# Windowed attention and two feed-forward layers on one core: a scheduled order of issue, 64-key softmax and a first block in halves

## The chip, the core and the metric

One core of a Trainium2 chip runs the whole program in a single launch. The metric is the device time of one execution in microseconds (us), lower is better. Engines are named as in the profile: PE is the tensor engine (PEld its weight loads), DVE the vector engine, ACT the scalar engine, POOL is GpSimd and SP issues most of the DMA transfers.

## What is computed

Three layers follow each other; all inputs and outputs are float32. `w_in` is 512 x 2048, `w_out` 2048 x 512, `w_a` and `w_b` 512 x 1536, and the last `w_out` 1536 x 512.

```python
# q, k, v: (4, 8, 576, 64); a query sees itself and the 63 keys before it
scores = q @ k^T / sqrt(64); scores outside 0 <= i - j < 64 are set to -1e9
attn   = softmax(scores); x = attn @ v, as 2304 tokens x 512
h = x @ w_in;  g = relu(h) ** 2;  x = g @ w_out            # layer 1
a = x @ w_a;   b = x @ w_b;       out = (a * b) @ w_out    # layer 2
```

## The kernel before, in words

**Precision.** Each factor of the two layers is held as a high and a low part in float32r. A product is therefore three matmuls, high x high, high x low and low x high (`mm3`, lines 169 to 172). Attention multiplies in plain float32; the trace shows two MATMUL records for each such matmul.

**Weights.** A tile of 128 x 512 weights arrives as 64-bit words (`w_load`, line 91), and `conv_1` to `conv_3` (lines 107 to 140) turn it into a high and a low part: three instructions on ACT (L119, L120, L138) and four on DVE (L126, L129, L130, L139). There are 68 tiles, two landing buffers, and 14, later 20, slots for converted tiles.

**Layers.** The 2304 tokens are in five blocks, `BLOCKS`, the first of 256 tokens and four of 512. Layer 1 uses its 16 units of 128 hidden columns in two groups (`G1`: 7 and 9), layer 2 its 12 units in two groups of 6 (`G2`). A group goes over all blocks before the next one begins, and a block's partial sums are kept in DRAM between the groups of a layer. `unit1` (line 462) is 12 matmuls into `ps_h`, relu and square on ACT and DVE (lines 363 to 366), and 12 matmuls into four accumulators `acc`. `unit2` (line 493) has two first products, `ps_a` and `ps_b`, and one second. A unit's second product is issued after the first product of the next unit (`pend`).

**Attention.** 128 tokens, a pair of chunks of 64, are one step `k` of `tick` (line 321), 18 in all. `att_scores` (line 229) multiplies 64 x 64 pieces of Q with 128 keys: four heads-pairs `hp`, two heads `j` in a pair and two chunks `e`, so 16 matmuls, into two buffers, one for each `j`. Consecutive matmuls go over the four combinations of `j` (rows 0 to 63 or 64 to 127 of the array) and `e` (its columns):

```python
        for hp in range(NHP):
            for j in range(2):
                r = slice(j * W, (j + 1) * W)
                for e in range(2):
                    o = slice(e * W, (e + 1) * W)
                    nc.tensor.matmul(
                        pss[j][o, hp, :],
                        q_t[c][r, e, hp, :],
                        k_t[c][r, hp, e * W:e * W + P],
```

The mask is added by a bf16 matmul for the first five pairs and on DVE after that. Maximum, exponential (ACT, L272, one instruction for each buffer and `hp`, over 128 keys) and division follow; `att_transpose` (line 289) turns each 128 x 128 piece with the array's transpose, 8 for a pair, copied to SBUF by ACT; `att_values` (line 300) is 16 matmuls of 64 columns.

**Order.** The code is written in a fixed interleaving: three parts of a tick and three parts of a conversion inside each unit. `plan1` (line 530) starts with three units of block 0, then block 1, then the rest of block 0, then blocks 2 to 4. Every engine works through its own queue in the order in which it was built.

Of the kernel before, what the change touches and what calls it, by code (L numbers as in the profile page):

```python
# [27 lines left out]
BLOCKS = [(0, 256), (256, 512), (768, 512), (1280, 512), (1792, 512)]  # L28
G1 = [range(0, 7), range(7, 16)]
G2 = [range(0, 6), range(6, 12)]  # L30
N0 = 3
ORDER = [1, 0, 2, 3, 4]
NPR = NCH // 2
PR = 2 * W
PR0 = BLOCKS[0][1] // PR
# [4 lines left out]
MASK_PE = 5  # L40
# [3 lines left out]
def kernel(  # L44
# [18 lines left out]
    raw_p = ctx.enter_context(tc.tile_pool(name="raw_p", bufs=2))  # L63
# [13 lines left out]


    src = {"in": w_in, "out": w_out, "a": w_a, "b": w_b, "out2": w_out2}
    seq = []  # L80
    last_use = {}
    for gi, (ph, us) in enumerate([(1, G1[0]), (1, G1[1]), (2, G2[0]), (2, G2[1])]):
        for u in us:
            for kind in ("in", "out") if ph == 1 else ("a", "b", "out2"):
                last_use[kind, u] = len(seq)
                seq.append((kind, u))
    n_load, n_conv = [0], [0]
    raw_t, wh, wl, slot_of = {}, {}, {}, {}
    free = [(ring_a, i) for i in range(N_A)]

    def w_load(k=1):
        for _ in range(k):
            if n_load[0] < len(seq) and n_load[0] < n_conv[0] + RAW:
                kind, u = key = seq[n_load[0]]
                n_load[0] += 1
                t = raw_p.tile([P, 512, 2], U32, tag="raw", name="raw", bufs=RAW)
                nc.sync.dma_start(out=t.rearrange("p f w -> p (f w)"), in_=src[kind][u].bitcast(U32))
                raw_t[key] = t
# [6 lines left out]
    cvs = [cv_p]  # L105

    def conv_1():
        if n_conv[0] == len(seq) or not free:
            return None
        key = seq[n_conv[0]]  # L110
        if key not in raw_t:
            w_load()
        n_conv[0] += 1
        slot_of[key] = free.pop(0)
        pool = cvs[n_conv[0] % len(cvs)]
        t = raw_t[key]
        a = pool.tile([P, 512], F32, tag="a", name="a")
        s = pool.tile([P, 512, 2], U16, tag="s", name="s")
        nc.scalar.activation(out=a, in_=t[:, :, 1].bitcast(F32), func=AF.Copy, scale=2.0 ** -112)  # L119
        nc.scalar.activation(out=s[:, :, 0], in_=t[:, :, 0], func=AF.Copy, scale=2.0 ** -29)  # L120
        return key, a, s

    def conv_2(key, a, s):
        t = raw_t.pop(key)
        au = a.bitcast(U32)
        nc.vector.tensor_scalar(  # L126
            out=s[:, :, 1], in0=t.bitcast(U16)[:, :, 3], scalar1=0x8000, scalar2=None, op0=ALU.bitwise_and
        )
        nc.vector.tensor_scalar(out=au, in0=au, scalar1=3, scalar2=None, op0=ALU.logical_shift_left)  # L129
        nc.vector.tensor_tensor(out=au, in0=au, in1=s.rearrange("p f w -> p (f w)").bitcast(U32), op=ALU.add)  # L130
        w_load()
        return key, a

    def conv_3(key, a):
        pool, i = slot_of[key]
        hi = pool.tile([P, 512], F32R, tag=f"wh{i}", name="wh")
        lo = pool.tile([P, 512], F32R, tag=f"wl{i}", name="wl")
        nc.scalar.copy(out=hi, in_=a)  # L138
        nc.vector.tensor_tensor(out=lo, in0=a, in1=hi.bitcast(F32), op=ALU.subtract)  # L139
        wh[key], wl[key] = hi, lo  # L140


    flow = {2: [], 3: []}

    def conv_step(step, k=1):
        for _ in range(k):
            if step == 1:
                r = conv_1()
                if r:
                    flow[2].append(r)  # L150
            elif flow[step]:
                r = flow[step].pop(0)
                if step == 2:
                    flow[3].append(conv_2(*r))
                else:
                    conv_3(*r)

    def need(key):
        while key not in wh:
            if not (flow[2] or flow[3]):  # L160
                conv_step(1)
            conv_step(2)
            conv_step(3)

    def w_done(kinds, u):
        for kind in kinds:
            free.append(slot_of.pop((kind, u)))
# [6 lines left out]
    def proj(ps, key, t):  # L174
        n = BLOCKS[t][1]
        h_, l_ = wh[key], wl[key]
        for kc in range(KC):
            c = slice(kc * P, (kc + 1) * P)
            mm3(ps[:, :n], h_[:, c], l_[:, c], xh[t][:, kc, :], xl[t][:, kc, :], kc == 0, kc == KC - 1)


    att = ExitStack()
    ld_p = att.enter_context(tc.tile_pool(name="ld_p", bufs=2))
# [7 lines left out]

    q_t, k_t, v_t = {}, {}, {}

    def ok(c):
        return 0 <= c < NPR

    def load_qk(c):
        if ok(c):  # L200
# [7 lines left out]
            if lo:  # L208

                nc.gpsimd.memset(k_t[c][:, :, :lo], 0.0)  # L210
# [445 lines left out]
```

## Time and profile before

| what | value |
|---|---|
| three runs | 957.81, 959.85, 960.30 us |
| median | 959.85 us |
| the profiled execution | 959.12 us, span 957.3 us |
| PE busy | 919.5 us (96%) |
| DVE busy, ACT busy | 433.1 us (45%), 382.6 us (40%) |
| DMA moved | 82.46 MB, mean 86 GB/s |

Times below are in one profiled execution, counted from the first instruction. Busy time is time in which an engine holds at least one instruction. Matmuls overlap each other on PE, so a busy PE can still be doing less than it could: the distance between two starts tells its pace.

### The profile page before, as it was taken

To read this page: it belongs to the slowest core of one execution; us is meant where nothing else is said; L and a number is where in the kernel's file an instruction comes from. 1 tells how busy PE (TensorE), PEld (TensorE's weight loads), DVE (VectorE), ACT (ScalarE), POOL (GpSimd) and SP (SyncE) were. 2 spreads that over 40 slices of the span, in tenths; PEclk is the share of its full clock that TensorE was granted. 3 is DMA by queue.
4 is the path that set the end of the run, shared out by engine and by line. 5 is a ranking of instruction groups with operands and counts; after the bars stand their busy time and mean duration, and the time that the engine had idled before them with its cause. 6 is when DMAs were issued, how large, how long until landed. Compare 5 with 4: busy or idle time off the path is not lost.

```text
span 957.3 us, 13306 instructions
## 1 busy us (share of the span) xinstructions
PE 919.5 (96%) x5314; PEld 764.6 (80%) x5314; DVE 433.1 (45%) x803; ACT 382.6 (40%) x866; POOL 2.0 (0%) x11
## 2 busy tenths in 40 slices
PE   4778999999999999999999999999999999999998
PEld 3666787778877898888888898888888888888886
DVE  3587865646885243242798122121484122121222
ACT  4787755556774232232686121111373111111111
POOL 0000000000000000000000000000000000000000
PEclk9899999999999999999999999999999999999999
DMA  6767734222655011010253010010252120002011
GB/s 179 215 197 224 214 116 126 69 89 88 219 175 173 1 39 45 1 45 1 82 193 131 2 45 23 1 45 0 88 166 86 46 83 27 24 22 66 8 48 45
DMA packets 59278, 82.46 MB, mean 86 GB/s; under 512 B 23248, under 2 KB 34896, under 8 KB 59216
## 3 DMA queue, kind: packets, MB, share of 16 engines
q1 hardware_dynamic: 58816, 81.41, 27.0%
q8 instruction: 42, 0.69, 0.3%
q10 hardware_dynamic: 400, 0.20, 0.1%
q14 instruction: 20, 0.16, 0.0%
HBM read 66.91 MB, written 14.68 MB: 85 GB/s over the span
## 4 chain that ended last, share of the span: by engine, by line
PE 79%; ACT 6%; DMA 6%; DVE 6%; SPq 1%; issue 1%; DVEq 0%; ACTq 0%
PE acc L170 10%; PE acc L171 10%; PE acc L172 10%; PE ps_b L170 5%; PE ps_a L170 5%; PE ps_b L171 5%; PE ps_b L172 5%; PE ps_a L172 5%; PE ps_a L171 5%; PE ps_h L170 5%; PE ps_h L172 5%; PE ps_h L171 5%; DMA raw<-in_w_in_dram 2%; ACT sm L272 2%; DMA raw<-in_w_out_dram 2%; PE ps_p L294 1%
## 5 line engine op out<-in xcount | busy, mean ns | idle before, releaser
L423 DVE TENSOR_TENSOR c<-a,ps_b 128x512 f32<-128x512 f32 (+1 forms) x60 | 38.0, 633 | 262.8 <-PE ps_b L172 262.8
L170 PE MATMUL ps_h<-xh,wh 128*128 128x512 f32 (+1 forms) x320 | 120.4, 376 | 1.4 <-DVE sm L259 1.4
L171 PE MATMUL acc<-lo,wh 128*128 128x512 f32 (+1 forms) x320 | 119.0, 373 | 1.7 <-DVE lo L366 1.7
L170 PE MATMUL acc<-hi,wh 128*128 128x512 f32 (+1 forms) x320 | 118.6, 374 | 1.9 <-ACT ev L389 1.8
L172 PE MATMUL ps_h<-xh,wl 128*128 128x512 f32 (+1 forms) x320 | 118.3, 370 | 1.2 <-DVE wl L139 1.2
L171 PE MATMUL ps_h<-xl,wh 128*128 128x512 f32 (+1 forms) x320 | 118.5, 370 | 0.0
L172 PE MATMUL acc<-hi,wl 128*128 128x512 f32 (+1 forms) x320 | 117.9, 369 | 0.0
L364 DVE TENSOR_TENSOR g<-r 128x512 f32<-128x512 f32 (+1 forms) x80 | 50.8, 635 | 121.5 <-ACT r L363 121.3
L419 ACT COPY a<-ps_a 128x512 f32<-128x512 f32 (+1 forms) x60 | 32.5, 542 | 176.1 <-PE ps_a L172 176.1
L363 ACT ACTIVATE r<-ps_h 128x512 f32<-128x512 f32 (+1 forms) x80 | 44.1, 551 | 134.3 <-PE ps_h L172 134.3
L171 PE MATMUL ps_a<-xl,wh 128*128 128x512 f32 (+1 forms) x240 | 88.3, 368 | 0.0
L172 PE MATMUL ps_a<-xh,wl 128*128 128x512 f32 (+1 forms) x240 | 88.3, 368 | 0.0
L171 PE MATMUL ps_b<-xl,wh 128*128 128x512 f32 (+1 forms) x240 | 88.3, 368 | 0.0
L172 PE MATMUL ps_b<-xh,wl 128*128 128x512 f32 (+1 forms) x240 | 88.3, 368 | 0.0
L170 PE MATMUL ps_b<-xh,wh 128*128 128x512 f32 (+1 forms) x240 | 88.3, 368 | 0.0
L170 PE MATMUL ps_a<-xh,wh 128*128 128x512 f32 (+1 forms) x240 | 88.2, 368 | 0.0
L348 ACT CAST hi<-c 128x512 fp32r<-128x512 f32 (+1 forms) x60 | 34.6, 577 | 127.7 <-DVE c L423 127.7
L170 PE MATMUL acc<-wh,hi 128*128 128x512 f32 x216 | 84.2, 390 | 0.0
L171 PE MATMUL acc<-wl,hi 128*128 128x512 f32 x216 | 84.2, 390 | 0.0
L172 PE MATMUL acc<-wh,lo 128*128 128x512 f32 x216 | 84.0, 389 | 0.0
L170 PEld LDWEIGHTS ps_h<-xh,wh 128*128 128x128 f32 x320 | 61.1, 191 | 13.0 <-DVE sm L259 2.5
L171 PEld LDWEIGHTS acc<-lo,wh 128*128 128x128 f32 x320 | 60.5, 189 | 13.7 <-DVE lo L366 3.7
(68 smaller groups left out, 1473.2 us busy)
## 6 DMA issues: line engine op xcount, KB each, us to landing
raw<-in_w_out_dram SPq DMA_DIRECT2D x28, 512.0 KB, 3.6
part<-ev SPq DMA_DIRECT2D x34, 256.0 KB, 2.6
pr<-part SPq DMA_DIRECT2D x34, 256.0 KB, 3.9
raw<-in_w_in_dram SPq DMA_DIRECT2D x16, 512.0 KB, 4.9
v_sb<-in_vwin_dram SPq DMA_DIRECT2D x32, 256.0 KB, 3.8
k_sb<-in_kT_dram SPq DMA_DIRECT2D x17, 384.0 KB, 4.1
raw<-in_w_a_dram SPq DMA_DIRECT2D x12, 512.0 KB, 3.5
raw<-in_w_b_dram SPq DMA_DIRECT2D x12, 512.0 KB, 3.5
```

The source lines that it names most:

```text
L170: nc.tensor.matmul(ps, ah, bh, start=first, stop=False)
L171: nc.tensor.matmul(ps, ah, bl, start=False, stop=False)
L172: nc.tensor.matmul(ps, al, bh, start=False, stop=last)
L272: nc.scalar.activation(out=p[:, hp, :], in_=sm[:, hp, :], func=AF.Exp, bias=nm[:, j, hp:hp + 1], scale=SCALE, accum_out=rs[:, j, hp:hp + 1],)
L294: nc.tensor.transpose(ps[:, hp * P:(hp + 1) * P], p[:, hp, :], ident)
L348: nc.scalar.copy(out=hi, in_=full)
L363: nc.scalar.activation(out=r, in_=ps, func=AF.Relu)
L364: nc.vector.tensor_tensor(out=g, in0=r, in1=r, op=ALU.mult)
L419: nc.scalar.copy(out=a, in_=pa[:, :n])
L423: nc.vector.tensor_tensor(out=c, in0=a, in1=pb[:, :n], op=ALU.mult)
```

## The change

- **Order of issue.** All work is now a list of steps (`plan.add`), each with an engine, an assumed duration, the steps it needs, a rank and the buffers that it takes or gives back. `Plan.issue` walks a schedule of these durations and then issues the steps in order of their scheduled start. The order is final: it is taken over instruction by instruction.
- **Attention on 64 keys.** Of the 128 keys that a chunk multiplies, a query sees exactly 64, one in each pair of places `p` and `p + 64`. `a_max` copies the seen one of each two over the other inside PSUM (`copy_predicated`, two instructions on 64 rows where a chunk begins a sequence). Maximum, exponential and division then handle 64 columns. To multiply with 128 rows of V again, `a_transpose` multiplies the 64 columns with the identity twice, into both halves of the rows, and `a_part`, on DVE, blanks with the mask `sees_T` what is not seen. The added mask is gone.
- **Loops of the matmuls.** `a_scores` now handles one head half `j` at a time, with `e` as the only thing that alternates; `a_transpose` consists of ordinary matmuls.
- **Blocks.** The blocks are 512, 512, 512, 512 and 256 tokens. The first three units of block 0 run in halves of 256 columns, and in its first group the square for `g` is on ACT.
- **Loads.** Q arrives in one transfer for a pair, with the zeros that stand between its heads (512 KB for 4 x 64 KB before); K of the first pair is issued by ACT.
- **Conversions** are steps of their own, with the rank of the tenth unit before the group that needs them.

```diff
-BLOCKS = [(0, 256), (256, 512), (768, 512), (1280, 512), (1792, 512)]
+BLOCKS = [(0, 512), (512, 512), (1024, 512), (1536, 512), (2048, 256)]
-        for hp in range(NHP):
-            for j in range(2):
-                r = slice(j * W, (j + 1) * W)
-                for e in range(2):
+    def a_scores(c, j):
+        r = slice(j * W, (j + 1) * W)
+        for hp in range(NHP):
+            for e in range(2):
+                nc.tensor.matmul(
+                    ps[e * W:(e + 1) * W, hp, :],
+                    T["q", c][r, e, hp, r],
+                    T["k", c][r, hp, e * W:e * W + P],
...
+            nc.vector.copy_predicated(
+                out=ps[o, :, W:],
+                mask=sees_l[o].unsqueeze(1).to_broadcast([n, NHP, W]),
+                data=out_of[o].unsqueeze(1).to_broadcast([n, NHP, W]) if none else ps[o, :, :W],
+            )
...
-                nc.tensor.transpose(ps[:, hp * P:(hp + 1) * P], p[:, hp, :], ident)
-            pT = s_p.tile([P, NHP, P], F32, tag="pT", name="pT", bufs=4)
-            nc.scalar.copy(out=pT.rearrange("p h q -> p (h q)"), in_=ps)
+            for e in range(2):
+                p = T["p", c][:, j * NHP + hp, :]
+                nc.tensor.matmul(ps[e * W:(e + 1) * W, hp, :], p, ident, start=True, stop=True)
+    def a_part(c, j):
+        nc.vector.tensor_tensor(
+            out=pT, in0=T["pp", c, j], in1=sees_T.unsqueeze(1).to_broadcast([P, NHP, P]), op=ALU.mult
+        )
...
+                opts.append((t, self.steps[i][5], i))
+                if opts:
+                    first = min(opts)[0]
+                    t, _, i = min((o for o in opts if o[0] <= first + 0.15), key=lambda o: (o[1], o[0]))
...
+        for _, _, i in sorted(order):
+            self.steps[i][3]()
...
+            add(("S", c, j), "PE", 0.3, f(a_scores, j), [("k", c), ("q", c)], rank, take="w" if c >= 2 else None)
...
+    for u in range(N0):
+        unit1(0, first[u], first, halves[1], nxt())
...
+        for u in us:
+            conv_ahead(rank[0] - 10)
```

How the order moves is shown at three places. On PE, the start of the program before (`ps_s` are scores, `ps_p` transposes, `ps_o` values, `ps_h` a first product, xN counts matmuls that follow each other):

```order
L243 MATMUL ps_s<-k_sb,q_sb 64x128 x11
L294 MATMUL ps_p<-ident,p 128x128 x8
L170 MATMUL ps_h<-xh_91,wh 128x256
L171 MATMUL ps_h<-xl_96,wh 128x256
L172 MATMUL ps_h<-xh_91,wl 128x256
```

These rows begin the first product of the kernel before, which stands behind the scores of five pairs, the transposes of four and the values of two. The start of the changed kernel on PE, from its first attention row (`ps_in` is a first product; `ps_m` turns the mask):

```order
L302 MATMUL ps_s<-k_sb,q_sb 64x128 x16
L605 MATMUL ps_m<-ident,sees 128x128
L302 MATMUL ps_s<-k_sb,q_sb 64x128 x16
L350 MATMUL ps_p<-ident,p 64x128 x16
L365 MATMUL ps_o<-pT,v_sb 64x64 x16
L350 MATMUL ps_p<-ident,p 64x128 x16
L365 MATMUL ps_o<-pT,v_sb 64x64 x16
L302 MATMUL ps_s<-k_sb,q_sb 64x128 x16
L170 MATMUL ps_in<-xh_91,wh 128x256
```

The first product now stands behind two complete pairs and the scores of a third; there are 16 matmuls of `ps_p` for a pair instead of 8. On PE inside block 1 of the changed kernel, between two units, the pieces of attention stand apart by head half:

```order
L350 MATMUL ps_p<-ident,p 64x128 x8
L302 MATMUL ps_s<-k_sb,q_sb 64x128 x8
L350 MATMUL ps_p<-ident,p 64x128 x8
L302 MATMUL ps_s<-k_sb,q_sb 64x128 x8
L170 MATMUL ps_in<-xh_93,wh 128x512
```

Before, such a place was 16 matmuls of `ps_s` in one run and 8 of `ps_p`. Over the whole queue there are 35 runs of 64-row or 64-column matmuls between other matmuls before, with 7 changes of kind inside them; now there are 37 runs with 33 changes inside.

On DVE, the changed kernel at the turn from layer 1 to layer 2, the last twelve rows ahead of the `lo` of a unit of the 256-token block (L211, L218, L223 and L233 are a conversion's four instructions, L490 the low part of layer 2's input):

```order
L211 TENSOR_SCALAR s<-raw 128x512
L218 TENSOR_SCALAR a<-a 128x512
L444 TENSOR_TENSOR g<-r 128x256
L211 TENSOR_SCALAR s<-raw 128x512
L223 ISA a<-a,s 128x1024
L218 TENSOR_SCALAR a<-a 128x512
L223 ISA a<-a,s 128x1024
L490 TENSOR_TENSOR xl_99<-pr,xh_94 128x512 x2
L233 TENSOR_TENSOR wl<-a,wh 128x512
L211 TENSOR_SCALAR s<-raw 128x512
L218 TENSOR_SCALAR a<-a 128x512
L452 TENSOR_TENSOR lo<-g,hi 128x256
```

Four tiles of weights are finished between the `lo` of the unit before and this one. In all, 17 tiles stand among the ten units around the turn to the second group of layer 1 (three of 512 columns, seven of 256), 11 among the nine units of 256 columns before layer 2, and 12 among the six before its second group. Before, the turns lay in blocks of 512 tokens with one or two tiles for a unit.

## Rows read from the trace of the kernel before

**Rows 1.** The page: busy time by engine; shares of the chain that ended last

```profile
PE 919.5 (96%) x5314; PEld 764.6 (80%) x5314; DVE 433.1 (45%) x803; ACT 382.6 (40%) x866; POOL 2.0 (0%) x11
...
PE 79%; ACT 6%; DMA 6%; DVE 6%; SPq 1%; issue 1%; DVEq 0%; ACTq 0%
```

**Rows 2.** The page: granted PE clock in 40 equal slices, in tenths

```profile
PEclk9899999999999999999999999999999999999999
```

**Rows 3.** Busy time by stretch: stretch, length, busy (xinstructions) of each engine, PE clock, DMA

```profile
0.00:40.00 40.00, 22.05 (x259) 15.24 (x260) 17.59 (x40) 22.02 (x81) 1.99 (x11) 0.95 0.71 195
...
150.00:270.00 120.00, 118.58 (x862) 95.91 (x861) 79.47 (x151) 72.46 (x180) 0.00 (x0) 1.00 0.39 126
...
270.00:300.00 30.00, 28.28 (x119) 21.57 (x118) 25.35 (x48) 23.25 (x39) 0.00 (x0) 1.00 0.62 201
...
400.00:500.00 100.00, 100.00 (x443) 82.79 (x442) 56.13 (x98) 47.95 (x80) 0.00 (x0) 1.00 0.22 71
```

**Rows 4.** The same from 0 to 150 us, line 308, then line 172 (PE, PEld)

```profile
0.00:150.00 150.00, 13.93 (x352) 12.09 (x352) 0.95 0.62 183
...
0.00:150.00 150.00, 39.69 (x116) 22.58 (x116) 0.95 0.62 183
```

**Rows 5.** Timeline of PE: start us, us, engine, line, operation, count; a pair's values and scores

```profile
174.02 0.39 PE L172 MATMUL ps_h<-xh,wl 128*128 128x512 f32 x1
...
174.34 1.15 PE L308 MATMUL ps_o<-pT,v_sb 128*64 128x64 f32 x32
...
175.42 0.50 PE L170 MATMUL acc<-hi,wh 128*128 128x512 f32 x1
...
178.05 0.39 PE L172 MATMUL acc<-hi,wl 128*128 128x512 f32 x1
...
178.37 1.10 PE L243 MATMUL ps_s<-k_sb,q_sb 64*64 64x128 f32 x32
...
179.40 0.50 PE L170 MATMUL ps_h<-xh,wh 128*128 128x512 f32 x1
```

**Rows 6.** Timeline of PE: a pair's eight transposes and what follows

```profile
195.90 1.03 PE L294 MATMUL ps_p<-ident,sm 128*128 128x128 f32 x8
...
196.69 0.48 PE L170 MATMUL ps_h<-xh,wh 128*128 128x512 f32 x1
```

**Rows 7.** Timeline of PE: a run of eight score records only

```profile
26.96 0.65 PE L243 MATMUL ps_s<-k_sb,q_sb 64*64 64x128 f32 x8
```

**Rows 8.** Timeline: the first scores, maxima and transposes, and the first product

```profile
6.87 1.98 PE L243 MATMUL ps_s<-k_sb,q_sb 64*64 64x128 f32 x32 [1.65 <-DMA k_sb<-in_kT_dram]
...
12.83 1.27 DVE L260 TENSOR_REDUCE nm<-ps_s 128x4 f32<-128x512 f32 x2
...
18.63 1.94 PE L294 MATMUL ps_p<-ident,p 128*128 128x128 f32 x8 [5.41 <-DVE p L285]
...
41.60 0.58 PE L170 MATMUL ps_h<-xh,wh 128*128 128x256 f32 x1
...
43.26 0.28 PE L170 MATMUL ps_h<-xh,wh 128*128 128x256 f32 x1
...
43.38 0.28 PE L171 MATMUL ps_h<-xl,wh 128*128 128x256 f32 x1
```

**Rows 9.** Timeline of DVE: instructions of conversions back to back

```profile
239.19 0.68 DVE L130 CUSTOM_DVE_ANT_0 a<-a,s 128x1024 uint16<-128x1024 uint16 x1
...
239.80 0.46 DVE L126 TENSOR_SCALAR s<-raw 128x512 uint16<-128x512 uint16 x1
...
240.14 0.41 DVE L129 TENSOR_SCALAR a<-a 128x512 uint32<-128x512 uint32 x1
```

**Rows 10.** Line 130, once for each tile: 250 to 300 us, then 400 to 500 us

```profile
250.00:300.00 50.00, 10.15 (x15) 1.00 0.61 205
...
L130 DVE CUSTOM_DVE_ANT_0 a<-a,s x11: 673/685/694, 471.3 to 498.9; 128x1024 uint16<-128x1024 uint16 x11
```

**Rows 11.** Timeline of PE: its last instruction

```profile
952.52 0.39 PE L172 MATMUL acc<-wh,lo 128*128 128x512 f32 x1
```

More of the change, by code (lines that the diff above doesn't have):

```diff
@@ L89 @@
[L89 to L140, printed above, removed]
@@ L143 @@
[L143 to L163, printed above, removed]
@@ L225 @@
+    x_of = {}
     for t, (t0, n) in enumerate(BLOCKS):
@@ L303, in att_values, with a_values @@
+    def a_values(c):
+        ps = T["o", c] = ps_w.tile([P, NHP, PR], F32, tag="w", name="ps_o")
         for hp in range(NHP):
@@ new lines, with mm_cost, u_proj @@
+    units = []
+    acc_free = [[("E", 1, 0), ("E", 1, 1)]]
+    def mm_cost(n):
+        return 0.2265 * n / 512 + (0.007 if n < 512 else 0)
+    def u_proj(name, key, t, cols):
+        n = cols.stop - cols.start
+        ps = T[name] = ps_w.tile([P, 512], F32, tag="w", name=f"ps_{key[0]}")[:, :n]
+        h_, l_ = T["wh", key], T["wl", key]
+        for kc in range(KC):
+            c = slice(kc * P, (kc + 1) * P)
+            mm3(ps, h_[:, c], l_[:, c], xh[t][:, kc, cols], xl[t][:, kc, cols], kc == 0, kc == KC - 1)
@@ new lines, in spill, with ev_, st_ @@
+    def spill(part, layer, t, count, k, rank, n):
+        ring = "ev" if layer == 1 and t < 3 else "pr"
+        acc_free[0] = []
+        for m in range(count):
+            def ev_(m=m):
+                ev = T["ev", layer, t, m] = pools[ring].tile([P, 512], F32, tag="pr", name="ev")[:, :n]
+                if m % 2:
+                    nc.vector.tensor_copy(out=ev, in_=T["acc"][m][:, :n])
+                else:
+                    nc.scalar.copy(out=ev, in_=T["acc"][m][:, :n])
+            def st_(m=m):
+                nc.sync.dma_start(out=part[t][:, m, :], in_=T["ev", layer, t, m])
+            add(("ev", layer, t, m), "DVE" if m % 2 else "ACT", 0.62, ev_,
+                [("O", k), "close" if ring == "pr" else None], rank + 1.6, take=ring)
+            add(("st", layer, t, m), "SP", 0.6, st_, [("ev", layer, t, m)], rank + 1.6, give=("ev", layer, t, m), size=0.26)
+            acc_free[0].append(("ev", layer, t, m))
@@ new lines, with nxt, tiles, conv_ahead @@
+    add("sees", "DVE", 0.2, c_sees, ["mask"], -3)
+    add("turn", "PE", 0.2, c_turn, ["sees", ("S", 0, 1)], 0, take="w")
+    add("sees_T", "DVE", 0.2, c_sees_T, ["turn"], 0, give="turn")
+    rank = [0]
+    def nxt():
+        rank[0] += 1
+        return rank[0]
+    def tiles(ph, u, r):
+        for kind in ("in", "out") if ph == 1 else ("a", "b", "out2"):
+            conv((kind, u), r)
+    todo_conv = [(1, u) for u in G1[1]] + [(2, u) for u in G2[0]] + [(2, u) for u in G2[1]]
+    def conv_ahead(r):
+        if todo_conv:
+            tiles(*todo_conv.pop(0), r)
@@ new lines @@
+    halves = [slice(0, 256), slice(256, 512)]
+    first = G1[0]
+    attention(0, nxt())
+    attention(1, nxt())
+    for u in range(N0):
+        tiles(1, u, nxt())
+        if u:
+            attention(1 + u, nxt())
+        unit1(0, first[u], first, halves[0], nxt())
+    for u in range(N0):
+        unit1(0, first[u], first, halves[1], nxt())
+        if u < N0 - 1:
+            tiles(1, N0 + u, nxt())
+    c = C0
+    for j, u in enumerate(first[N0:]):
+        if N0 + j >= 2 * N0 - 1:
+            tiles(1, u, rank[0] - 2)
+        attention(c, nxt())
+        c += 1
+        unit1(0, u, first, slice(0, 512), nxt())
@@ L593, in _lay_out @@
+    with tc.manual_schedule():
+        plan.issue()
 def _lay_out(inputs):
```

730 lines of the change are left out of this document (385 added, 345 removed).

## The prediction, made before the result was known

> **What bounds the kernel now.** I read the page's busy shares first. PE is busy 96% of the span, DVE and ACT 45% and 40%, and PE holds 79% of the chain that ended last [rows 1]. A busy PE may still run below its pace, so next I took the table of stretches and counted instructions. From 400 to 500 us, 443 matmuls of 512 columns start, one each 0.2257 us [rows 3]; this is the pace of PE where nothing disturbs it. A matmul of 256 columns takes 0.12 us from start to start [rows 8].
>
> With these units I ask how much of each stretch PE used. By 150 us, line 172 has run 116 times, so 348 matmuls of the two layers have run, three for each [rows 4]: 168 of 256 columns (the seven units of block 0) and 180 of 512, or 20.2 + 40.6 = 60.8 us. Line 308 has run 352 times, 32 for a pair, so 11 pairs are done, and 12 or 13 have had their other parts: some 12 pairs. A pair's values take from 174.25 (174.02 and one unit of 0.23) to 175.42, and the matmul behind them lasts 0.50 instead of 0.39, so 1.28 us in all. The scores take from 178.28 to 179.40 and the same 0.11, so 1.23 us [rows 5]. The transposes take 0.79, and the next matmul is 0.09 longer: 0.88 us [rows 6]. That is 3.39 us a pair, 40.7 us for 12, and 2.3 us for ten bf16 mask matmuls at about a unit each. **PE has done 104 us of work in 150 us: 46 are lost.** In the first 40 us PE has only 259 records and no product of the layers: the first one starts at 41.60 [rows 3, 8]. From 150 to 300 us about 6 us more are lost: 119 matmuls of 0.2257 are 26.9 of the 30 us from 270 on, and the count of the 120 us before it leaves about 3 [rows 3]. After that PE is dense, up to its last start at 952.52; 4.6 us follow up to the end of the span at 957.3 [rows 11]. So the span is some 900 us of PE work and 57 us of loss, nearly all of it early. A better order can only win from these 57, and every PE microsecond that is added late counts in full.
>
> **What the change adds on PE.** Three groups of rows give a price by column. Eight transposes move 8 x 128 = 1024 columns, one at a time over the whole array, in 0.87 us: 0.85 ns a column [rows 6]. Values are 32 records of 64 columns on half of the array's columns. Two at a time at 0.85 ns, their 2048 columns are 0.87 us, and 0.41 is left for changing over. Scores are 32 records of 128 columns on a quarter of the array, twice the columns in the same time [rows 5]. That fits only four at a time: 4096 x 0.85 / 4 = 0.87, and 0.36 for changing over. Four at a time is not given to every run of scores: a run of only 8 records lasts 0.65 us, against 1.10 for 32 [rows 5, 7]. Its own starts spread over about 0.38 us, three steps of 0.11 where four at a time would need one.
>
> The changed kernel multiplies one `j` after the other. Only `e` alternates, so two pieces of the array are used and the other two are idle: 1.74 us a pair for the scores, 0.87 more. The 8 transposes become 16 ordinary float32 matmuls. That is 32 records of 128 columns on half of the array, two at a time as in the values: 1.74 us, again 0.87 more. For 18 pairs this is 15.7 + 15.7 = **31.4 us**. [...]
>
> Changes of mode come on top. The queue has 37 runs instead of 35 (2 x 0.36) and 33 changes of kind inside them instead of 7. At 0.15 each (what is left between a run's 0.36 to 0.41 and its return to 128 x 128 tiles, 0 to 0.4 at the bounds) that is 3.9, so 4.6 us. [...] Halving three units' products replaces 72 matmuls of 0.2257 by 144 of 0.12: +1.0. The mask matmuls go: -2.3. PE's work rises by **34.7 us** to about 935.
>
> **What it removes.** The first product depends on two pairs and two tiles. I walk it through. Scores started at 6.87 before, behind seven issues on one queue; now Q and K come by one issue each on two queues, so about 5. At the slow pace of the start, where 32 records took 1.98 at four at a time [rows 8], scores of both pairs end near 12. For pair 0, maximum (copy 0.4 to 0.7, reduction 0.4, both bounded by DVE rows of 0.41 and 0.68 [rows 9], and the scaling) and exponentials run beside the later scores, and the division ends near 13. Transposes, masked copies, values and the two parts of `x` take it to near 19.5; pair 1 follows by 4, and the weights' `wl` behind it on DVE makes **24 us** (20 to 28) instead of 41.6. By then PE has done about 12 us of work, so 12 are lost. From there on DVE has four maxima ahead of the first `lo`, so the second product waits some 2 us, and the next three units wait 0.5 us each. Then PE has more to do than DVE: to the end of block 0, PE has eight pairs at 5.5 and 40 us of units, 84 us, and DVE some 70 (14 tiles at 1.9, eight pairs at 4.7, units). I take 18 us lost by the end of block 0, for the 46 of before: **-28 us** (-20 to -33). The clock, at 0.8 to 0.9 of full in the second slice for the time that PE stood idle [rows 2], is part of these 46.
>
> DVE and ACT get no price of their own. The halved exponentials and the copies moved from ACT to DVE lie beside PE work that is longer now; where a pair's chain is on the path, in the first 24 us, the walk has it. The Q transfer is twice as large, but in one piece, and the stretch from 150 us on has 0.39 of the DMA share in use [rows 3]; if it is late, it is late in the first 24 us, inside the walk's range.
>
> **The turns between groups** are new losses. The last block of a group has 256 tokens, so the time in which its slots come free is halved, and the conversions have a lower rank, so a better place, than the ten units before the turn. They stand in DVE's queue between the units' own instructions, which cannot pass them. A tile takes DVE about 1.9 us from start to start: 0.61 + 0.34 are seen, the other two 0.33 and 0.61 like them [rows 9]. First turn: 17 tiles (32.3) with ten units' `g` and `lo` (3 x 1.2 + 7 x 0.8) and two copies make 42.3 us on DVE, against 3 x 5.42 + 7 x 2.88 = 36.4 on PE. Second: 11 tiles, nine units and eight more instructions, 32.9 against 25.9. Third: 12 tiles, six units, two copies, 28.8 against 25.5. Together 16 us. PE's order lets first products run up to three ahead, 4.3 us a turn, so 2 + 3 + 0 = 5 is the low bound. With tiles at the pace of the earlier turn, 15 in 50 us [rows 10], the bound above is 44; at the other rate there, 11 in 27.5 us, it is 12. I take 11, near that nearest row. The 6 us lost from 150 to 300 fall away: **+5 us**.
>
> At the end, the last unit has 256 columns and its last product waits for `g`, the high and the low part, with no other product between: **+1.6 us** (0 to 2).
>
> Sum against the profiled execution (959.12, its span and 1.8 us around it): 959.1 + 34.7 - 28 + 5 + 1.6 = 972.4. The median of the runs, 959.85, is 0.7 above it, inside the spread of the runs. **I forecast 972 us, slower by 1.3%.**
>
> **Rivals.** (1) *The waits are absorbed, faster:* the run-ahead of PE's queue hides the turns (0 instead of 11), and after the first product nothing waits, so only 12 us are lost early instead of 18: 972.4 - 17 = 955. It decides if all losses together stay below 21 us (with 935 of work and 1.8 outside the span). For: three first products stand ahead of the second at the first turn. Against: they cover 4.3 us a turn. (2) *Four at a time after all:* the two halves of a pair's scores often stand next to each other and use other rows, so they run together, and 15.7 us go: 956.7. [...] Only four neighbours that alternate were seen four at a time [rows 5], and the short run was not [rows 7]; so small. (3) *Early waits stay:* the fixed order makes engines wait for each other as before, and 13 more of the old 46 us stay: 985. Against: PE is now the longer one there. (4) *The turns go at the pace of 250 to 300 us:* 18 us more, 990. (5) *Nothing moves:* what is won early pays just for PE's work, and the end is not seen: 960.
>
> **Chances.** The forecast, own range 961 to 983, has 0.54 (same 0.05, slower 0.49). Rival 1 has 0.18 (faster 0.16, same 0.02), rival 2 0.08 (faster 0.05, same 0.03), rival 3 0.10 and rival 4 0.08 (slower), rival 5 0.02 (same). Within 0.3%, 2.9 us, is what a measurement here can't tell from no change. So faster 0.21, same 0.12, slower 0.67. The range 953 to 990 leaves out the lower part of rival 1 and the upper part of rival 4.
>
> **What would show it.** Scores of one `j`, 16 records, should take about 0.9 us between first start and end of pace, and 16 records of the new transposes as much. The first `ps_in` should start at 20 to 28 us. Around the turns, the instructions of PE in a 10 us stretch should fall, with second products waiting for `lo` on DVE. I am wrong if the scores of a pair still take 1.2 us, if PE is dense through all three turns, or if the first product starts after 30.

## The result, and the profile after

The changed kernel takes **972.58 us** (median of four runs, 971.80 to 974.25), the kernel before 959.81 beside it. The ratio is 1.0139, 95% interval 1.0119 to 1.0160: slower by 1.4%, as forecast (972, slower). The profiled execution took 971.99 us, its span 970.2. That is 12.9 us more than the span of before. I first show the rows, then test which term of the sum was really there.

The page of the changed kernel: busy time by engine, granted clock in 40 slices, shares of the chain [rows 1, 2]:

```profile
PE 943.5 (97%) x5809; PEld 790.8 (82%) x5809; DVE 442.3 (46%) x851; ACT 357.1 (37%) x846; POOL 1.0 (0%) x8
...
PEclk9999999999999999999999999999999999999999
...
PE 87%; DMA 5%; ACT 4%; DVE 4%; issue 1%; SPq 0%; ACTq 0%; DVEq 0%
```

PE's share of the chain has grown from 79 to 87%: there is less waiting, and more work. The start, timeline of PE (columns as in [rows 5]), to be read against [rows 8]:

```profile
5.70 2.89 PE L302 MATMUL ps_s<-k_sb,q_sb 64*64 64x128 f32 x32 [5.70 <-DMA k_sb<-in_kT_dram]
8.52 0.47 PE L605 MATMUL ps_m<-ident,sees 128*128 128x128 f32 x1
...
14.49 3.68 PE L350 MATMUL ps_p<-ident,p 128*64 128x128 f32 x32 [2.68 <-ACT p L331]
17.93 0.42 PE L365 MATMUL ps_o<-pT,v_sb 128*64 128x64 f32 x2
...
26.00 0.39 PE L170 MATMUL ps_in<-xh,wh 128*128 128x256 f32 x1
```

The first product starts at 26.00 instead of 41.60. Where PE is dense, from 86 us on, the same view gives the prices of the new pieces, from the first start to the start of what follows:

```profile
86.64 1.59 PE L302 MATMUL ps_s<-k_sb,q_sb 64*64 64x128 f32 x32
88.16 0.50 PE L170 MATMUL ps_in<-xh,wh 128*128 128x512 f32 x1
...
91.15 1.09 PE L350 MATMUL ps_p<-ident,p 128*64 128x128 f32 x16
92.17 0.50 PE L170 MATMUL acc<-hi,wh 128*128 128x512 f32 x1
...
95.11 1.97 PE L350 MATMUL ps_p<-ident,p 128*64 128x128 f32 x32
97.01 1.09 PE L302 MATMUL ps_s<-k_sb,q_sb 64*64 64x128 f32 x16
98.03 1.09 PE L350 MATMUL ps_p<-ident,p 128*64 128x128 f32 x16
```

Scores of one `j` (16 records) take 1.02 us, two halves next to each other (32 records) only 1.52, and four at a time in the kernel before 1.03 [rows 5]. Transposes take 1.02 for half a pair and 1.90 for a pair; eight took 0.79 before [rows 6]. On PE 12 pairs have their scores together and 6 apart, 7 have their transposes together and 11 apart. So PE's work rose by 12 x 0.49 + 6 x 1.01 = **11.9** for the scores and 7 x 1.11 + 11 x 1.25 = **21.5** for the transposes. With +1.0 for the halves and -2.3 for the mask matmuls that is 32.1 us. The span rose by 12.9, so 19.2 us of loss (waits, and time at a slower pace) went.

Most went early. Up to 150 us line 172, the scores, the transposes and the values stand as follows [rows 4]:

```profile
0.00:150.00 150.00, 40.84 (x118) 22.28 (x118) 1.00 0.59 195
...
0.00:150.00 150.00, 23.46 (x384) 19.55 (x384) 1.00 0.59 195
...
0.00:150.00 150.00, 26.71 (x384) 22.43 (x384) 1.00 0.59 195
...
0.00:150.00 150.00, 14.59 (x352) 12.79 (x352) 1.00 0.59 195
```

That is 354 matmuls (144 of them of 256 columns, 64.7 us), 12 pairs of scores and of transposes, 11 of values, and 0.11 for each return to the layers: some 122 us of work, 28 lost. The same prices give 50 lost before. How much of these 22 us comes from the order, from the softmax on 64 keys or from the loads was not parted; the halves alone were tested (below).

The new loss at a turn is seen once, at the second turn (busy time from 500 to 520 us, columns as in [rows 3]), then the timelines of PE and of ACT there:

```profile
500.00:520.00 20.00, 16.12 (x102) 14.51 (x101) 18.00 (x38) 16.08 (x31) 0.00 (x0) 0.91 0.62 201
```

```profile
507.24 0.39 PE L170 MATMUL ps_in<-xh,wh 128*128 128x256 f32 x1 [1.70 <-ACT r L437]
...
511.12 0.50 PE L170 MATMUL ps_a<-xh,wh 128*128 128x512 f32 x1 [2.19 <-ACT r L437]
```

```profile
507.99 0.69 ACT L203 ACTIVATE a<-raw 128x512 f32<-128x512 f32 x1 [0.80 <-DMA raw<-in_w_a_dram]
508.58 0.76 ACT L208 ACTIVATE s<-raw 128x512 uint16<-128x512 uint32 x1
509.21 0.65 ACT L203 ACTIVATE a<-raw 128x512 f32<-128x512 f32 x1
509.77 0.77 ACT L208 ACTIVATE s<-raw 128x512 uint16<-128x512 uint32 x1
510.41 0.39 ACT L448 ACTIVATE hi<-r 128x256 fp32r<-128x256 f32 x1
510.71 0.36 ACT L437 ACTIVATE r<-ps_in 128x256 f32<-128x256 f32 x1
```

PE waits for a PSUM buffer that `r` on ACT empties, and ahead of `r` in ACT's queue stand two tiles' conversions, the first of which still waits for its DMA. Of the 6 us lost here (some 80 matmuls of 256 columns and 20 of 512 are about 14 of the 20 us), 3.9 are these two waits. Behind the second the trace grants half the clock for 3.4 us, where matmuls of 512 columns start 0.43 us apart instead of 0.23; by estimate, half of the 3.4, that is 1.7 us more.

### The profile page after: what moved, and what is told of

It reads as the page before. It is cut to its first block, busy times and chain, and to the rows that moved or that the text cites. A ratio compares the mean times of both kernels' runs of the same rounds, so it can differ in the third digit from the quotient of the medians.

```text
span 970.2 us, 14298 instructions
## 1 busy us (share of the span) xinstructions
PE 943.5 (97%) x5809; PEld 790.8 (82%) x5809; DVE 442.3 (46%) x851; ACT 357.1 (37%) x846; POOL 1.0 (0%) x8
## 4 chain that ended last, share of the span: by engine, by line
PE 87%; DMA 5%; ACT 4%; DVE 4%; issue 1%; SPq 0%; ACTq 0%; DVEq 0%
PE acc L170 11%; PE acc L171 11%; PE acc L172 11%; PE ps_in L170 6%; PE ps_in L172 6%; PE ps_in L171 5%; PE ps_a L170 5%; PE ps_a L171 5%; PE ps_a L172 5%; PE ps_b L170 5%; PE ps_b L171 5%; PE ps_b L172 5%; PE ps_p L350 3%; PE ps_s L302 2%; DMA raw<-in_w_out_dram 2%; PE ps_o L365 2%
## 5 line engine op out<-in xcount | busy, mean ns | idle before, releaser
L544 DVE TENSOR_TENSOR g<-r,ps_b 128x512 f32<-128x512 f32 (+1 forms) x60 | 38.0, 633 | 256.5 <-PE ps_b L172 256.3
L170 PE MATMUL ps_in<-xh,wh 128*128 128x512 f32 (+1 forms) x332 | 122.3, 368 | 4.2 <-ACT r L437 1.7
L548 ACT CAST hi<-g 128x512 fp32r<-128x512 f32 (+1 forms) x60 | 34.6, 576 | 249.1 <-DVE g L544 246.0
L170 PE MATMUL acc<-hi,wh 128*128 128x512 f32 (+1 forms) x332 | 121.7, 367 | 0.0
L172 PE MATMUL ps_in<-xh,wl 128*128 128x512 f32 (+1 forms) x332 | 120.2, 362 | 0.7 <-DVE wl L233 0.6
L171 PE MATMUL ps_in<-xl,wh 128*128 128x512 f32 (+1 forms) x332 | 120.1, 362 | 0.0
L452 DVE TENSOR_TENSOR lo<-g,hi 128x512 fp32r<-128x512 f32 (+1 forms) x83 | 51.3, 618 | 97.2 <-ACT hi L448 95.0
L448 ACT ACTIVATE hi<-r 128x512 fp32r<-128x512 f32 (+1 forms) x83 | 47.7, 575 | 119.9 <-PE acc L172 119.1
L170 PEld LDWEIGHTS ps_in<-xh,wh 128*128 128x128 f32 x332 | 62.6, 189 | 16.8 <-ACT r L437 2.1
L170 PEld LDWEIGHTS acc<-hi,wh 128*128 128x128 f32 x332 | 62.6, 188 | 11.9 <-issue 2.1
```

The costliest lines, as they stand in the source:

```text
L448: nc.scalar.activation(out=T["hi", k], in_=T["r", k], func=AF.Square)
L452: nc.vector.tensor_tensor(out=T["lo", k], in0=T["g", k], in1=T["hi", k].bitcast(F32), op=ALU.subtract)
L544: nc.vector.tensor_tensor(out=T["g", k], in0=T["r", k], in1=T["B", k], op=ALU.mult)
L548: nc.scalar.copy(out=T["hi", k], in_=T["g", k])
```

## Experiments: the price of the scores alone

**In the kernel before, one `j` after the other.** The loops are exchanged, nothing else.

```diff
-        for hp in range(NHP):
-            for j in range(2):
+        for j in range(2):
+            for hp in range(NHP):
```

> The kernel before with one edit: the two outer loops of the scores are exchanged, so that all matmuls of one j go before those of the other; same instructions, same order otherwise. Theory (only neighbours in the queue run together): a pair's scores take 0.87 us more wherever PE is the bound; the first twelve pairs stand in a stretch with 46 us of loss, where up to all of it is hidden, so 965 to 976, and a pair's scores between the same neighbours in the trace 1.9 to 2.1 us instead of 1.12. Rival (the array finds four pieces to run whatever the order in the queue): 960, and 1.1 to 1.2 us in the trace.

Measured: 960.61 us, ratio 0.9995 (0.9971 to 1.0019): no change, the time that the rival gave. The timeline of PE in this run:

```profile
181.19 1.59 PE L243 MATMUL ps_s<-k_sb,q_sb 64*64 64x128 f32 x32
182.71 0.50 PE L170 MATMUL ps_h<-xh,wh 128*128 128x512 f32 x1
```

The pace is a third answer: 1.52 us, neither the 1.03 of the rival nor the 1.9 of the theory. Where the halves of a pair stand next to each other in the queue, the second costs only half as much as the first, 0.50 against 1.02 us; whether part of it runs beside the first, no run parts (last section). Up to 8.8 us more PE work (18 x 0.49) then cost nothing: in the kernel before, the waits take it in.

**In the changed kernel, scores as one step that takes both buffers.**

```diff
-            add(("S", c, j), "PE", 0.3, f(a_scores, j), ...)
+        add(("S", c, 1), "PE", 0.6, f(a_scores), [("k", c), ("q", c)], rank, take="w2" if c >= 2 else None)
```

> The changed kernel, but the scores of a pair are one step that takes both buffers and goes over j inside hp again, so that four neighbours use the four quarters of the array. Theory (pace: one j alone leaves half of the array idle): the scores of a pair fall by 0.87 us, 18 pairs give 15.7 us back, and some fewer changes of kind another 1; 956 us (953 to 960), scores of a pair about 1.2 us from first start to the next work. Rival A (the waits take it back: the plan's order or DVE sets the pace of block 0 and 1): within 3 us of the changed kernel, 970 to 975, with idle time of PE before the first products and the transposes grown by about what the scores lose. Rival B (two halves of a pair ran together in the changed kernel already): no change, and scores of one j that have their neighbour next to them take less than 0.7 us each in the changed kernel's trace.

Measured: 978.34 us, ratio 1.0179 (1.0148 to 1.0210): slower still, outside all three expectations. The scores do take 1.03 for a pair, 11.9 us less in all. But the plan, given another step, wrote another order, and PE's timeline has waits that the changed kernel does not have:

```profile
54.61 0.58 PE L171 MATMUL ps_in<-xh,wh 128*128 128x256 f32 x1 [5.03 <-ACT p L333]
...
62.55 1.86 PE L367 MATMUL ps_o<-pT,v_sb 128*64 128x64 f32 x29 [4.42 <-DVE pT L356]
```

Such a run can't price the scores, since it changes the order as well. So the next one keeps every queue's order.

**The same, with every queue as in the changed kernel.** Where both halves of a pair already stand next to each other on PE (12 pairs), their matmuls alternate.

```diff
-        for hp in range(NHP):
-            for e in range(2):
+        for hp in range(NHP):
+            for i in range(2) if c in plan.pairs else [j]:
...
+                for e in range(2):
```

> The changed kernel with every engine's queue in exactly its order; only where both scores of a pair already stand next to each other on PE (12 of the 18 pairs) their 16 matmuls go over j inside hp, so that four neighbours use four quarters. It tells the pace apart from the order, which the run with one step for both scores changed as well. Theory: the pace is worth 0.87 us a pair wherever PE is the bound, and nothing in the first 60 us, where DVE is; 8 of the 12 pairs come later, so 7 us: 965.5 (962 to 968). Rival A: any PE time saved in attention comes back as waits (and as a lower granted clock behind them), whatever the order: 970 to 975. Rival B: every one of the 12 counts: 962 or less.

Measured: 970.03 us, ratio 1.0105 (1.0080 to 1.0129): about 3 us faster than the changed kernel, outside the theory's range and at the edge of rival A's. The two intervals overlap a little, so the gain is only just clear of the noise. The timeline shows the pace that was meant:

```profile
87.02 1.10 PE L316 MATMUL ps_s<-k_sb,q_sb 64*64 64x128 f32 x32
88.06 0.50 PE L181 MATMUL ps_in<-xh,wh 128*128 128x512 f32 x1
```

12 x 0.49 = 5.9 us of work went, and the profiled span fell by 4.0. The expectation had the saving of a pair too large (0.87), because it took 1.90 for scores that are together.

## Experiments: the transposes, and a clock that falls

**The array's transpose again, ordered by the plan; then with the scores of the second run above.**

```diff
-                nc.tensor.matmul(ps[e * W:(e + 1) * W, hp, :], p, ident, start=True, stop=True)
+            nc.tensor.transpose(ps[:, hp, :], p2, ident)
```

> The changed kernel, but the division writes each head's 64 columns twice, and eight transposes of 128 x 128 by the array's transpose stand for the sixteen ordinary float32 matmuls. Theory (price by columns): the transposes fall from 1.74 to 0.87 us a pair, so 15.7 us back, and their changes of kind go, since 128 x 128 is the layers' own kind (up to 36 runs at 0.15 to 0.36, 5 us or more): 951 us (948 to 958). DVE has about 0.6 us more for each pair, 11 us in all, in a stretch where it is busy less than two thirds. Rival A (DVE's queue is the bound of the first 230 us): the longer division comes back as waits, 11 us or more, so 960 to 972. Rival B (the transposes were hidden behind other waits): no change, 970 to 975.

> Both edits of the two runs before together. If PE's work is the bound wherever they act, the gains add: 15.7 + 15.7 and 4 for changes of kind make 937 us (932 to 945), faster than the kernel before by some 2%. If waits take the place (DVE and ACT in the first 150 us), the sum falls short by the share of the early stretch, where eleven of the eighteen pairs stand: 945 to 958.

Measured: 974.51 us, ratio 1.0143 (1.0111 to 1.0175), and 966.00 us, ratio 1.0058 (1.0031 to 1.0085). The first lies in the range of its rival B, the second above both of its ranges. By the rows above they take 21.5 and 33.4 us of work from PE, and the spans (974.4 and 964.0) moved by +4.2 and -6.2. Again the order is another one, so these two were repeated with every queue as in the changed kernel:

> The changed kernel with every queue in its order, the transposes by the array's transpose, eight of 128 x 128 for a pair; the exponentials go into one half of a double tile, and the division is done twice (one more DVE instruction of about 0.7 us for a pair). Theory: 0.87 us and one or two changes of kind (0.15 to 0.36) a pair where PE is the bound, some 14 pairs behind 60 us: about 16 us less, 957 (952 to 962). Rival A: what is saved comes back as waits, for DVE is longer by 13 us as well: 968 to 976, with the waits of the transposes for the division grown in the first 100 us and a lower clock there.

> Both of the two edits before, every queue in its order. Theory: the two gains behind 60 us add, 7 + 16: 949.5 (944 to 957), faster than the kernel before. Rival A (waits and clock take it): above 962, as when the plan ordered the same two edits by itself.

Measured: 961.55 us, ratio 1.0019 (1.0002 to 1.0035), and 962.72 us, ratio 1.0035 (1.0015 to 1.0055). The first is at the upper edge of its theory's range, the second is rival A's. The transposes are worth 1.2% of the time, the scores on top of them nothing that can be told. Of the 21.5 and 27.4 us of work the medians show 11.0 and 9.9, the spans of the profiled executions 7.8 and 8.6. Where did the rest go? First the busy table of the changed kernel, in two stretches, then in small steps that of the run with the transposes (the last three columns are granted clock, DMA share, GB/s):

```profile
20.00:40.00 20.00, 16.09 (x229) 13.56 (x225) 17.06 (x39) 13.86 (x51) 0.00 (x0) 1.00 0.71 252
40.00:60.00 20.00, 16.37 (x219) 14.83 (x217) 18.67 (x46) 15.08 (x46) 0.00 (x0) 1.00 0.75 246
```

```profile
28.00:32.00 4.00, 2.19 (x28) 1.58 (x25) 3.59 (x12) 3.97 (x15) 0.00 (x0) 0.87 0.71 229
32.00:36.00 4.00, 3.47 (x15) 3.17 (x16) 3.25 (x9) 3.21 (x15) 0.00 (x0) 0.50 0.95 305
36.00:40.00 4.00, 4.00 (x26) 3.67 (x26) 2.40 (x4) 2.75 (x16) 0.00 (x0) 0.50 0.45 182
40.00:44.00 4.00, 3.21 (x19) 2.59 (x16) 2.99 (x9) 2.68 (x6) 0.00 (x0) 0.50 0.00 0
44.00:48.00 4.00, 4.00 (x43) 3.66 (x43) 3.68 (x8) 0.60 (x2) 0.00 (x0) 0.50 0.35 119
```

In this execution of the changed kernel the granted clock stays at 1.00. With the quick transposes it falls to 0.50 after a stretch in which PE was busy 2.19 of 4 us, and stays there for 16 us. The timeline of that run shows what it means, 0.21 us from start to start instead of 0.12 [rows 8]:

```profile
32.14 0.41 PE L172 MATMUL acc<-hi,wl 128*128 128x256 f32 x1
32.35 0.41 PE L170 MATMUL acc<-hi,wh 128*128 128x256 f32 x1
```

At this pace, 1.75 times the time at half the clock, the most that such a stretch costs is by estimate its length times what the clock lacks: over 20 us steps up to 120 us, the columns of clock add up to 10.2 us here, 12.0 with the scores as well, and 22.0 in the plan's own order of both. In the table below that is set beside what came back in the profiled execution, the work saved by the prices above less the fall of the span against 970.2. The last two columns are for all executions: what came back by the medians (against 972.58), and what the mean clock lacks over the whole span, on average, above the 4.1 us of the changed kernel. The medians are of different rounds, in which that of the kernel before moved by up to 1.5 us.

| run | work saved on PE | span | came back | clock lacks, to 120 us | came back, medians | clock lacks more, mean |
|---|---|---|---|---|---|---|
| scores, same order | 5.9 | 966.2 | 1.9 | 1.8 | 3.3 | 0.5 |
| transposes, same order | 21.5 | 962.4 | 13.7 | 10.2 | 10.5 | 2.1 |
| both, same order | 27.4 | 961.6 | 18.8 | 12.0 | 17.5 | 7.0 |
| scores, plan's order | 11.9 | 976.1 | 17.8 | 13.4 | 17.7 | 10.1 |
| transposes, plan's order | 21.5 | 974.4 | 25.7 | 12.0 | 23.4 | 11.7 |
| both, plan's order | 33.4 | 964.0 | 27.2 | 22.0 | 26.8 | 14.9 |

What the clock lacks is an upper bound, as PE has pauses in those stretches too. Its real price can be read from two executions. The run with the other block order (below) has the changed kernel's queues in the attention stage, but from 32.9 us its clock was at half for 6.8 us, which lacks 3.4 us. These are the starts of the 73rd matmul of the layers, first in the changed kernel, then in that run:

```profile
54.57 0.28 PE L170 MATMUL acc<-hi,wh 128*128 128x256 f32 x1
```

```profile
56.49 0.28 PE L170 MATMUL acc<-hi,wh 128*128 128x256 f32 x1
```

The 3.4 us cost 1.9, little more than half. At that price, an estimate from the two executions, the clock accounts for 5 to 6 of the 13.7 us that came back in the profiled execution with the transposes. That execution was also the slowest of its ten and had the lowest mean clock (0.988; the others 0.991 to 0.997). By the last two columns the clock is about 1 of 10.5 us there, and less than a third in every row. So the fall of the clock is real, but most of what came back, as the remainder, is waits for DVE and ACT.

Where it came back can be seen by the same count. The 349th matmul of the layers stands behind the transposes of twelve pairs, the 701st behind those of all eighteen. First the changed kernel, then the run with the transposes in its order:

```profile
148.62 0.50 PE L170 MATMUL ps_in<-xh,wh 128*128 128x512 f32 x1
...
262.50 0.39 PE L171 MATMUL acc<-lo,wh 128*128 128x512 f32 x1
```

```profile
147.41 0.48 PE L170 MATMUL ps_in<-xh,wh 128*128 128x512 f32 x1
...
254.31 0.39 PE L171 MATMUL acc<-lo,wh 128*128 128x512 f32 x1
```

Of the 14.1 us saved in the first twelve pairs 1.2 have arrived at 148 us. Of the 7.4 us saved in the last six, 7.0 have arrived.

**Is it the clock? The slow transposes put back for the first six pairs only.**

```diff
-            nc.tensor.transpose(ps[:, hp, :], p, ident)
+            if c >= OLD:
+                nc.tensor.transpose(ps[:, hp, :], p.rearrange("p e w -> p (e w)"), ident)
+            for e in range(2) if c < OLD else ():
+                nc.tensor.matmul(ps[e * W:(e + 1) * W, hp, :], p[:, 0], ident, start=True, stop=True)
```

> The run with the array's transposes in the changed kernel's order, but its first six pairs keep the sixteen slow matmuls and the single division. In that run the granted clock of PE was about 0.5 between 32 and 48 us and 0.8 between 56 and 64; in the changed kernel it is 1.00 there. Theory (the clock): PE, with more to do early, keeps its clock as the changed kernel does, some 10 us come back there, and the saving of the first six pairs, 6 to 7 us, is missed by nobody, since it lay beside idle time: twelve pairs at 0.87 and one or two changes of kind, 14 us below the changed kernel, so 958.5 (956 to 961), and a clock of 0.9 or more in 28 to 64 us. Rival (the double division and waits behind it): the first six pairs had a real gain and the later ones have the loss, so 964 to 968, slower than the run with all pairs.

Measured: 960.22 us, ratio 1.0015 (1.0001 to 1.0029), inside the theory's range. From 20 to 60 us the table now reads:

```profile
20.00:40.00 20.00, 17.15 (x217) 14.58 (x213) 17.26 (x40) 14.04 (x51) 0.00 (x0) 0.91 0.76 252
40.00:60.00 20.00, 16.17 (x217) 14.69 (x216) 18.55 (x45) 15.01 (x45) 0.00 (x0) 1.00 0.76 249
```

The clock is back but for some 4 us. These six pairs cost PE 21.5 - 14.6 = 6.9 us more than in the run with all quick ones, yet the time is the same (ratios 1.0015 and 1.0019), and the span is 4.2 us shorter. Of 14.6 us saved, 2.6 came back. So 7 us of PE work in that stretch cost nothing that these runs can tell. The clock alone can't pay for them. In the two profiled executions it lacks 1.8 us instead of 10.2, some 5 us at the price above; but over all executions the mean clock lacks 3.9 us (twelve of this run) instead of 6.2 (ten of the other), about 1 us. The rest lies in waits. The six pairs also divide once instead of twice, 0.7 us less on DVE for each, and PE's waits for the division up to 120 us (in all, how often, the longest) are, first with all quick transposes, then here:

```profile
PE ps_p L350 <- DVE p L342: 4.5, 3, 3.4
```

```profile
PE ps_p L352 <- DVE p L343: 1.1, 2, 0.9
```

In the changed kernel they are 0.2 us. How much of this the second division makes and how much the lower clock, the run doesn't part. A kernel that keeps PE busy with empty work would, and was not tried.

## Experiments: halves, turns, and a faster version

**Whole units for the first three units of block 0.**

```diff
-        if u:
-            attention(1 + u, nxt())
-        unit1(0, first[u], first, halves[0], nxt())
-    for u in range(N0):
-        unit1(0, first[u], first, halves[1], nxt())
-        if u < N0 - 1:
-            tiles(1, N0 + u, nxt())
+        if u < 2:
+            attention(2 + u, nxt())
+        unit1(0, first[u], first, slice(0, 512), nxt())
+    for u in range(N0 - 1):
+        tiles(1, N0 + u, nxt())
```

> The changed kernel with the three first units of block 0 whole, 512 columns, instead of in halves; the plan orders the rest by the same rules. Theory (the halves let products start when two of four pairs are done): the first product starts behind the fourth pair's transposes, at 33 to 42 us instead of 26; PE's work falls by 1.0, PE idles 5 to 12 us more by 80 us, with a low clock behind it: 977 to 984. Rival (the other pairs' work fills the time): 971 to 974, the halves are worth nothing.

Measured: 981.06 us, ratio 1.0221 (1.0191 to 1.0251): the halves are worth 8.5 us, in the theory's range. The first product comes at 48.86, later than I expected, since PE waits for the division of the third pair and then for the `xh` of the fourth:

```profile
32.83 3.68 PE L350 MATMUL ps_p<-ident,p 128*64 128x128 f32 x32 [5.53 <-DVE p L341]
...
48.86 0.79 PE L170 MATMUL ps_in<-xh,wh 128*128 128x512 f32 x1 [4.79 <-ACT xh L375]
```

**The turns, in two ways: later ranks for the conversions, and another order of the blocks.**

```diff
-            conv_ahead(rank[0] - 10)
+            conv_ahead(rank[0] - 2)
```

> The changed kernel, with one number changed: the conversions of the tiles of the next groups get the rank of the units around the turn minus 2 instead of minus 10, so they stand later in DVE's and ACT's queues. Theory of the prediction (the conversions stand ahead of the units' own instructions on DVE and hold second products up): the loss of 6 us at 500 to 520 us falls to 2 or 3, so 968.5 (967 to 970). Rival (what holds PE there is the tiles themselves, which cannot come before the old ones are used up, and the block order that gave 5.2 us moved that point): 971 to 975, or slower, since the first tiles of the next group come later still.

```diff
-        for t in range(len(BLOCKS)):
+        for t in (0, 4, 1, 2, 3):
```

> The changed kernel, but in the last three groups the block of 256 tokens is the second and not the last, so that a block of 512 stands at the second and third turn between groups and at the end. Theory (the short block halves the time in which slots of weights come free, and leaves the last product uncovered): the 6 us lost around the second turn, 500 to 520 us, fall to about 2 and the end loses 1.6 less, so 967 (964 to 970), with PE dense through the stretch and its clock full. Rival (the conversions of eleven tiles behind a group's last use of its slots take that long whatever the block): 972 to 974.

Measured: 966.31 us, ratio 1.0059 (1.0042 to 1.0076), and 967.35 us, ratio 1.0074 (1.0055 to 1.0094): 6.3 and 5.2 us faster than the changed kernel, the first just below its theory's range, the second in it. Busy time at the second turn, first with late conversions, then with the other block order:

```profile
500.00:520.00 20.00, 20.00 (x137) 18.57 (x137) 18.73 (x42) 16.61 (x33) 0.00 (x0) 1.00 0.47 145
```

```profile
500.00:520.00 20.00, 20.00 (x90) 16.57 (x89) 15.73 (x31) 14.57 (x25) 0.00 (x0) 1.00 0.45 156
```

Either edit alone makes PE dense there. The stall needs both, conversions placed ahead of the units' own instructions and a short block that gives PE little to do meanwhile. The end is another matter. With a block of 512 last, the last product still waits, as the timeline of the run with the other block order shows:

```profile
959.18 0.50 PE L170 MATMUL acc<-wh,hi 128*128 128x512 f32 x1 [1.50 <-ACT hi L548]
```

So the size of the last block is not what uncovers it; the order is, which has no other product in between.

**All that helped, in one kernel:** slow transposes for the first six pairs, quick ones for the rest, alternating scores for seven later pairs, and the other block order.

> The run before, and in addition the block of 256 tokens second in the last three groups, and the scores of pairs 6, 7, 9, 10, 12, 14 and 16 over j inside hp. Theory: the three gains lie in different stretches and add: 958.5 - 5.2 (the block order, as measured) - 7 x 0.87 = 947 (944 to 953), faster than both kernels. Rival (beyond the transposes any PE time saved behind 60 us comes back as waits for DVE, as the run with both edits showed no more than the one with transposes alone): 953 (951 to 957).

Measured: **953.94 us, ratio 0.9944 (0.9924 to 0.9964)**: faster than both kernels, by 0.6% and by 1.9%. It missed the theory's range (944 to 953) by one and met the rival's 953. The saving of the seven pairs was overrated, 7 x 0.49 = 3.4 instead of 6.1, and 3.4 us of clock were missing before 60 us in the profiled execution. The rival's reason, that nothing of the scores' saving arrives behind 60 us, holds in part: from the 73rd to the 701st matmul of the layers this run takes 195.2 us, the run before 196.7, so 1.5 of the 3.4 us arrived.

## Why the prediction came out right, point by point

- **PE's work, forecast +34.7, by rows +32.1.** Right in size, wrong in its parts. For scores the sum had 15.7, and they cost 11.9: "Only `e` alternates, so two pieces of the array are used" holds for halves that stand apart (1.02 each), not for halves that follow each other (1.52 for both). By the price rival 2 was in part right, for the twelve pairs that are together. Their 1.52 us lie between the 1.03 of four that alternate and the 2.04 of two halves apart. The transposes were sized 15.7 plus most of 4.6 for changes of kind; 21.5 by rows. A change of kind was priced at 0.15 us: two halves apart cost 0.14 more than two together for transposes, but 0.52 for scores. The sum had twice the old time (1.74 against 0.87); the rows give 2.4 to 2.6 times (1.90 and 2.04 against 0.79).
- **"Every PE microsecond that is added late counts in full"** held, and its other side was missed: early ones count for little or nothing. Of the transposes' work 7.0 of 7.4 us counted in the last six pairs and 1.2 of 14.1 in the first twelve. One `j` at a time cost the kernel before nothing. The sum booked the change's early PE work in full and made up for it in the fall of the early loss.
- **Early loss, forecast 46 to 18 (-28); by rows 50 to 28 (-22).** The first product came at 26.0, forecast 24 (20 to 28). The walk was right in kind. The rest was not parted; it lies in the first 20 us, where PE ran at little more than half of its later pace (below), and from 20 to 60 us, where DVE is busy 17 to 19 of 20 us.
- **The turns, +5, and the end, +1.6:** together 12.9 - 32.1 + 22 = about +3. The second turn lost 6 us, the other two hardly anything, where the sum had 11 for three. The wait is not the one named, "second products waiting for `lo` on DVE": it is first products waiting for `r` on ACT, where the conversions stand too. That they stand ahead is shown by the later ranks. The end lost 1.2 (1.30 from the last `ps_b` start to the next, less 0.12), not through the block's size.
- **The sum:** 34.7 - 28 + 6.6 = 13.3 was forecast for a span that rose by 12.9; the rows give 32 - 22 + 3. The time was met, and to 1 us by luck, because terms that were off by 3 to 6 us had opposite signs. Rival 1 fell with the second turn, rivals 3 to 5 by the early rows and the single short turn.

## What to carry to other kernels

Price added work by where it stands: in a stretch where an engine waits anyway it can be free, and taking it away there can bring next to nothing (here 1.2 of 14.1 us). Before a profiled execution is read as typical, set its time and its clock beside those of the other executions. When testing one part of a change in a kernel whose order is planned, keep every queue in its order, or the run measures the order. Where a plan gives work ahead of its time a better place than the work of the moment, look at every engine that shares that queue, not only the busiest.

## What the runs showed of the hardware that was not expected

- Runs on different quarters of the array went faster where they met in the queue: 32 score records take 1.52 us as two halves in a row, 1.03 when all four alternate, 2.04 as two halves apart. Each further half in a row added only 0.50: 16, 32 and 48 records last 1.09, 1.59 and 2.09 us in the changed kernel, and 64 last 2.59 in the run with whole units (its line stands below). Two halves of the transposes, which use the same parts of the array, save only 0.14. Whether the halves of the scores run beside each other or share a start that costs 0.5 us, no run parts.

```profile
24.71 2.59 PE L302 MATMUL ps_s<-k_sb,q_sb 64*64 64x128 f32 x64
```

- The table's 1.00 for the clock of the first 20 us is no reading: the changed kernel's trace has no record of the clock before 19.97 us. The pace there is lower than later: 32 score records take 2.82 us from 5.70 (1.52 later), 32 transposes 3.44 from 14.49 (1.90 later). These are 1.86 and 1.81 times, near the 1.75 at a granted 0.50 above (0.21 against 0.12 from start to start); what clock was granted there, the trace does not show.
- The clock later fell behind a thin stretch in some executions and not in all: to 0.50 behind 2.19 of 4 us busy in the run with the transposes in the changed kernel's order, while the changed kernel kept 1.00 behind 2.43 of 4 us, from 28 to 32 us, and the run with the other block order, whose queues are the changed kernel's in the attention stage, had 0.83 from 20 to 40 us where that one had 1.00. What made it fall, no run parts.
